# Grouped-query attention, 16 x 32 heads: 8 KB key pieces, score rows by key half, minima and sums joined on GpSimd

## The chip, the core and the metric

One core of one Trainium2 chip. The metric is device time of one execution in microseconds (us); the kernel before takes 350.31 us (median of 3 runs, 349.84 to 350.39). The core has TensorE (PE; PEld is its weight load), VectorE (DVE), ScalarE (ACT), GpSimd (POOL) and SyncE (SP), which issues all DMAs here. Each engine runs its own instructions in order; engines wait for each other by semaphores.

## The reference, cut to what matters

```python
B, Hq, Hkv, Sq, Sk, D = 16, 32, 8, 16, 2048, 128        # all bf16
k = jnp.repeat(k, rep, axis=1); v = jnp.repeat(v, rep, axis=1)     # rep = 4
scores = jnp.einsum("bhqd,bhkd->bhqk", q, k) * D ** -0.5
p = softmax(scores, axis=-1)
return jnp.einsum("bhqk,bhkd->bhqd", p, v)
```

There are 128 (batch, key head) groups. Each has 64 query rows (4 heads by 16 positions), 2,048 keys and 2,048 values of 128 numbers. K and V are 64 MB each, Q and the output 2 MB each; every byte of K and V is used once.

## The kernel before, in words

Work goes by *pairs* of groups, p = 0 to 63 (`NP`), 2 MB of K and V each. A pair passes through these steps; `[p % 2]` and the like are rotating buffers.

- **SP** issues, for t = 0, 1, 2 ...: `load_k(t)` (1 MB; for pair 0 two halves), a chunk of Q every eighth t (`load_q`, 256 KB, the queries of 8 pairs), `load_v(t - VLAG)`, `store(t - SLAG)` (L192-201). A K load waits until DVE has transposed the pair six before (`NK` = 6 buffers), a V load until the product eight before is done (`NV` = 8), a store until its output is normalised.
- **DVE** `kt` (L301): a 32x32-block transpose of K, two instructions of 128x1024 4-byte words a pair (a word is two bf16 numbers).
- **POOL** `spread` (L134) rearranges a chunk of Q once per 8 pairs; PE `queries` (L243) transposes it, ACT evacuates it to QT (L343); POOL copies one pair's part to Qs (L151).
- **PE** `scores` (L211): 32 matmuls of 32 rows by 64 columns into S_ps, which is all of four PSUM banks. PSUM rows 0-63 are group 0's queries, rows 64-127 group 1's; columns are keys.
- **DVE** Sneg (L324): one instruction over 128x2048 scales the scores by -scale, writes them to SBUF and leaves each row's minimum in nbias. Then `recip` of the row sum of the pair before.
- **ACT** exp (L353): one instruction over 128x2048 writes bf16 weights to P and the row sum to rowsum.
- **PE** `transposes` (L231): eight 128x128 transposes of P as 4-byte words; **ACT** copies them to PT in two halves (L363).
- **PE** `product` (L255): 16 matmuls with 128x128 weights and 256 moving columns (V of both groups), so half of each result (rows of one group by V of the other) is not used; **ACT** norm (L375) scales the two useful quarters, 64 rows each.

PE's order in a step p is `scores(p + 1)`, `product(p - PVLAG)`, `transposes(p)`, and in four of eight steps one unit of `queries` of the next chunk. ACT's order is exp p, norm p - PVLAG, the two PT copies of p, and a query evacuation where there is one. At the end, three products are left after the last scores; they go to the free S_ps banks.

Of the kernel before, what the change touches and what calls it, by code (L numbers as in the profile page):

```python
# [17 lines left out]
VLAG = 4  # L18
PVLAG = 3
# [4 lines left out]
def bass_standalone__gqa_softmax__sampling_kernel(  # L24
# [5 lines left out]
):  # L30
    B, Hq, Sq, D = q.shape
# [5 lines left out]
    J = Sk // 128  # L37
    assert J == 16 and NP % 8 == 0
# [8 lines left out]
    ident = sb("ident", [128, 128], BF16)  # L47
    ident4 = sb("ident4", [128, 128], F32)
    Kn = [sb(f"Kn{i}", [128, 2, J * 128], BF16) for i in range(NK)]
    Vb = [sb(f"Vb{i}", [128, 2, J, 128], BF16) for i in range(NV)]  # L50
    KT = [sb(f"KT{i}", [128, 2, J * 64], F32) for i in range(NKT)]
    Qn = [sb(f"Qn{i}", [128, 8, 128], BF16) for i in range(NQ)]
    Q4 = sb("Q4", [128, 8, 2, 4, 64], BF16)
    QT = [sb(f"QT{i}", [128, 4, 1024], BF16) for i in range(2)]
    Sneg = [sb(f"Sneg{i}", [128, Sk], F32) for i in range(2)]
    P = [sb(f"P{i}", [128, Sk // 2], F32) for i in range(2)]
    PT = [sb(f"PT{i}", [128, J // 2, 128], F32) for i in range(NPT)]
    Osb = [sb(f"O{i}", [128, 128], BF16) for i in range(NO)]
    nbias = sb("nbias", [128, NP], F32)
    rowsum = sb("rowsum", [128, NP], F32)  # L60
    rrec = sb("rrec", [128, NP], F32)

    Qs = [sb(f"Qs{i}", [128, 4, 128], BF16) for i in range(2)]
# [13 lines left out]
    sem_q4 = sem("sem_q4")  # L77
    sem_max = sem("sem_max")
    sem_rec = sem("sem_rec")
# [12 lines left out]
    kf = k.rearrange("b h s d -> (b h) (s d)").rearrange("g (a x) -> a g x", a=128)  # L92
# [3 lines left out]
    act_prog = []  # L96
    for i in range(4):
        act_prog.append(("qe", 0, i))
    for p in range(NP - 1):
        act_prog.append(("exp", p))  # L100
        if p >= PVLAG:
            act_prog.append(("norm", p - PVLAG))
        for h in range(2):
            act_prog.append(("pe", p, h))
        c, i = divmod(p, 8)
        if c + 1 < NQC and 2 <= i < 6:
            act_prog.append(("qe", c + 1, i - 2))
    act_prog.append(("exp", NP - 1))
    for p in range(NP - 4, NP - 2):
        act_prog.append(("norm", p))  # L110
    for h in range(2):
        act_prog.append(("pe", NP - 1, h))
    for p in range(NP - 2, NP):
        act_prog.append(("norm", p))

# [3 lines left out]

    def o_ap(p):  # L120
        if p < NP - 3:
            return O_ps[:, 0:256]
        x = p - (NP - 3)
        return S_ps[:, 512 * x:512 * x + 256]

    with nc.Block() as block:

        @block.gpsimd
        def _(gp):
            gp.iota(iota_t[:, :], [[1, 128]], base=0, channel_multiplier=-1).then_inc(sem_id, 1)  # L130
            gp.wait_ge(sem_id, 1)
            gp.tensor_scalar(ident[:, :], iota_t[:, :], 0.0, None, op0=ALU.is_equal).then_inc(sem_id, 1)
            gp.tensor_scalar(ident4[:, :], iota_t[:, :], 0.0, None, op0=ALU.is_equal).then_inc(sem_id, 1)
            def spread(c):  # L134
                gp.wait_ge(sem_q[c % NQ], 16 * (c // NQ + 1))
                if c >= 1:
                    gp.wait_ge(sem_tq, 4 * c)
                src = Qn[c % NQ][:, :, :].rearrange("p j (b x) -> p (j b) x", b=2)
                gp.tensor_copy(  # L139
                    Q4[:, :, :, :, :].rearrange("p j b r x -> p (j b) r x"),  # L140
                    src.unsqueeze(2).to_broadcast([128, 16, 4, 64]),
                ).then_inc(sem_q4, 8)

            spread(0)
            for p in range(NP):
                c, i = divmod(p, 8)
                if i == 0:
                    gp.wait_ge(sem_evq, 8 * c + 8)
                if p >= 2:
                    gp.wait_ge(sem_s, p - 1)  # L150
                gp.tensor_copy(Qs[p % 2][:, :, :], QT[c % 2][:, :, 128 * i:128 * (i + 1)]).then_inc(sem_qs, 1)  # L151
                if i == 0 and c + 1 < NQC:
                    spread(c + 1)

        @block.sync
        def _(sp):
            def load_k(p):
                s = p % NK
                if p >= NK:
                    sp.wait_ge(sem_kt, p - NK + 1)  # L160
                if p == 0:
                    for g in range(2):
                        sp.dma_start(Kn[s][:, g, :], kf[:, g, :]).then_inc(sem_k0[g], 16)
                else:
                    sp.dma_start(Kn[s][:, :, :], kf[:, 2 * p:2 * p + 2, :]).then_inc(sem_k[s], 16)

            def load_v(p):
# [7 lines left out]
                for x in range(2):  # L175
                    dst = Vb[s][:, :, 8 * x:8 * (x + 1), :].rearrange("a g j d -> a g (j d)")
                    src = vf[:, 2 * p:2 * p + 2, 1024 * x:1024 * (x + 1)]
                    sp.dma_start(dst, src).then_inc(sem_vl[x], 16)

            def load_q(c):  # L180
                s = c % NQ
                if c >= NQ:
                    sp.wait_ge(sem_q4, 8 * (c - NQ + 1))
# [3 lines left out]
            def store(p):  # L187
                s = p % NO
                sp.wait_ge(sem_nm, p + 1)
                sp.dma_start(of[128 * p:128 * (p + 1), :], Osb[s][:, :]).then_inc(sem_o[s], 16)  # L190

            for t in range(NP + SLAG + 1):  # L192
                if t < NP:
                    load_k(t)
                for c in range(NQC):
                    if t == max(0, 8 * c - QLEAD):
                        load_q(c)
# [8 lines left out]
        def _(pe):  # L206
# [4 lines left out]
            def scores(p, i, first=False):  # L211
# [4 lines left out]
                kt = KT[i % NKT][:, :, :].bitcast(BF16).rearrange("p g (t b x e) -> p g b e t x", t=J // 2, b=2, e=2)  # L216
                qs = Qs[i % 2]
                for acc in range(4):
                    b, e = divmod(acc, 2)
                    for r in range(4):  # L220
                        rows = slice(32 * r, 32 * (r + 1))
                        for g in range(2):
                            ins = pe.matmul(  # L223
                                S_ps[64 * g:64 * (g + 1), 512 * r:512 * (r + 1)],
                                qs[rows, acc, 64 * g:64 * (g + 1)],
                                kt[rows, g, b, e, :, :],
# [16 lines left out]
            def queries(p, i, first=False):  # L243
                if i == 0:
                    pe.wait_ge(sem_q4, p + 8)
                if i or not first:
                    pe.wait_ge(sem_evq, p + 2 * i)
                dst = stage_ap(2).bitcast(BF16)
                src = Q4[:, :, :, :, :].rearrange("p j b r (c e) -> p j b e (r c)", e=2)
                b, e = divmod(i, 2)  # L250
                for j in range(8):
                    ins = pe.transpose(dst[:, 128 * j:128 * (j + 1)], src[:, j, b, e, :], ident[:, :])  # L252
                ins.then_inc(sem_tq, 1)

            def product(p, i, out, tail=False, last=False):  # L255
# [5 lines left out]
                elif not isinstance(p, int) or p >= 1:  # L261
                    pe.wait_ge(sem_nm, p)
                pt = PT[i % NPT][:, :, :].bitcast(BF16).rearrange("p t (q e) -> p t e q", e=2)
                for j in range(J):
                    if last and j % 8 == 0:
                        pe.wait_ge(sem_vl[j // 8], 16)
                    ins = pe.matmul(  # L267
                        out, pt[:, j // 2, j % 2, :], Vb[i % NV][:, :, j, :],
                        start=(j == 0), stop=(j == J - 1),
                    )  # L270
                ins.then_inc(sem_pv, 1)

            def step(base, i, more=True):
                p = base + i
                if more:
                    scores(p + 1, i + 1)
                if not isinstance(base, int) or p >= PVLAG:
                    product(p - PVLAG, i - PVLAG, o_ap(0))
                transposes(p, i, first=isinstance(base, int) and p == 0)
                if (not isinstance(base, int) or base + 8 < NP) and 2 <= i < 6:  # L280
                    queries(base + 8, i - 2)

            for i in range(4):
                queries(0, i, first=True)
            scores(0, 0, first=True)
            for i in range(8):
                step(0, i)
            with pe.Fori(8, NP - 8, 8) as base:
                for i in range(8):
                    step(base, i)  # L290
            for i in range(7):
                step(NP - 8, i)
            for p in range(NP - 4, NP - 2):
                product(p, p, o_ap(p), tail=(p >= NP - 3))
            transposes(NP - 1, 7)
            for p in range(NP - 2, NP):
# [3 lines left out]
        def _(dve):  # L300
            def kt(p, g):  # L301
                if p == 0:
                    dve.wait_ge(sem_k0[g], 16)
                else:
                    dve.wait_ge(sem_k[p % NK], 16 * (p // NK + (1 if p % NK else 0)))
                ins = dve.transpose(  # L306
                    KT[p % NKT][:, g, :].rearrange("p (t b a e) -> p t e b a", t=J // 2, b=2, e=2),
                    Kn[p % NK][:, g, :].bitcast(F32).rearrange("p (t e b c) -> p t e b c", e=2, b=2, c=32),
                )
                if g == 1:  # L310
                    ins.then_inc(sem_kt, 1)

            def recip(p):
                dve.wait_ge(sem_exp, p + 1)
                dve.reciprocal(rrec[:, p:p + 1], rowsum[:, p:p + 1]).then_inc(sem_rec, 1)  # L315

            for p in range(2):
                for g in range(2):
                    kt(p, g)
            for p in range(NP):  # L320
                dve.wait_ge(sem_s, p + 1)
                if p >= 2:
                    dve.wait_ge(sem_exp, p - 1)
                dve.tensor_scalar(  # L324
                    Sneg[p % 2][:, :], S_ps[:, :], -scale, None,
                    op0=ALU.mult, op1=ALU.min, accum_out=nbias[:, p:p + 1],
                ).then_inc(sem_max, 1)
                if p >= 1:
                    recip(p - 1)
                if p + 2 < NP:  # L330
                    for g in range(2):
                        kt(p + 2, g)
            recip(NP - 1)
# [72 lines left out]
```

## Time and profile before

| | |
|---|---|
| median of 3 runs | 350.31 us |
| the profiled execution: time / span | 350.13 us / 348.3 us |
| busy: PE, DVE, ACT, POOL | 270.0, 294.8, 279.5, 68.5 us |
| moved by DMA | 138.70 MB, mean 398 GB/s |
| granted TensorE clock | full in all 40 slices |
| DVE, mean ns: K transpose 128x1024 / Sneg 128x2048 | 1223 / 2256 |
| ACT, mean ns: exp 128x2048 / PT copy 128x512 / query evacuation 128x1024 / norm 64x128 | 2003 / 595 / 1031 / 361 |

The span is what the profiler sees of one execution; the execution's own time is 1.8 us longer. A group's row gives the line, engine and operation, destination <- source with their shapes, the count, then total busy time and mean duration, then the idle time that the engine had just before these instructions and what ended it. "DMA share" is the mean busy share of the 16 DMA engines; it reads above 1 when packets overlap.

### The profile page before, as it was taken

How to read it: one execution, taken by the hardware profiler on the slowest of the kernel's cores; microseconds unless marked ns; L12 is line 12 of the kernel's file. 1: busy time of each engine (PE TensorE's matmuls, PEld its weight loads, DVE VectorE, ACT ScalarE, POOL GpSimd, SP SyncE). 2: the span in 40 equal slices, each digit the busy share in tenths (PEclk: the TensorE clock that was granted, in tenths of full speed). 3: DMA queues.
4: the chain of work that ended last, by engine and by line, in shares of the span. 5: the costliest groups of instructions: out<-in, count | busy, mean ns of one | idle time of the engine just before them, and what ended most of it. 6: DMA issues, size and time to landing. Idle time of an engine off the chain costs nothing.

```text
span 348.3 us, 9331 instructions
## 1 busy us (share of the span) xinstructions
PE 270.0 (78%) x3840; PEld 199.8 (57%) x3840; DVE 294.8 (85%) x320; ACT 279.5 (80%) x417; POOL 68.5 (20%) x79
## 2 busy tenths in 40 slices
PE   0338789988898989888867886778867868767776
PEld 0215566666666666666646655556645656556565
DVE  2229999999999999988989889889889879889850
ACT  0326899989998999899877997689986898777775
POOL 3251106110421124110331104201051101101000
PEclk9999999999999999999999999999999999999999
DMA  7999999999999999999999999999999999999991
GB/s 272 417 410 409 408 408 405 412 410 410 410 413 413 413 410 411 412 410 414 410 413 413 412 412 412 412 413 413 412 411 413 412 412 414 413 409 414 410 384 45
DMA packets 45494, 138.70 MB, mean 398 GB/s; under 512 B 11424, under 2 KB 11424, under 8 KB 45472
## 3 DMA queue, kind: packets, MB, share of 16 engines
q1 hardware_dynamic: 45472, 138.42, 100.0%
q8 instruction: 11, 0.18, 0.2%
q14 instruction: 11, 0.09, 0.1%
HBM read 136.31 MB, written 2.10 MB: 397 GB/s over the span
## 4 chain that ended last, share of the span: by engine, by line
DMA 40%; DVE 26%; issue 14%; PE 8%; SPq 6%; ACT 5%; POOL 1%; ACTq 0%; POOLq 0%
DMA Kn<-in_k_dram 38%; DVE KT L306 15%; DVE Sneg L324 11%; PE O_ps L267 3%; ACT P L353 3%; SPq L190 3%; SPq L173 3%; PE S_ps L223 2%; DMA Qn<-in_q_dram 2%; PE S_ps L267 2%; PE ST_ps L239 1%; ACT PT L363 1%; POOL Q L139 1%; ACT O L375 0%; DVE rrec L315 0%
## 5 line engine op out<-in xcount | busy, mean ns | idle before, releaser
L306 DVE STREAM_TRANSPOSE KT<-Kn 128x1024 f32<-128x1024 f32 x128 | 151.6, 1223 | 29.8 <-DMA Kn<-in_k_dram 29.8
L324 DVE TENSOR_SCALAR_CACHE_REDUCE Sneg<-S_ps 128x2048 f32<-128x2048 f32 x64 | 144.4, 2256 | 12.8 <-PE S_ps L223 12.8
L353 ACT ACTIVATE P<-Sneg,nbias 128x2048 bf16<-128x2048 f32 x64 | 128.2, 2003 | 11.9 <-DVE Sneg L324 10.9
L267 PE MATMUL O_ps<-Vb,PT 128*128 128x256 bf16 x976 | 117.2, 273 | 0.0
L223 PE MATMUL S_ps<-KT,Qs 32*64 32x512 bf16 x2048 | 73.6, 400 | 53.4 <-DVE Sneg L324 46.3
L267 PEld LDWEIGHTS O_ps<-Vb,PT 128*128 128x128 bf16 x976 | 90.6, 98 | 36.0 <-issue 25.0
L151 POOL COPY Qs<-QT 128x512 bf16<-128x512 bf16 x64 | 38.8, 613 | 234.5 <-PE S_ps L223 159.0
L239 PE MATMUL ST_ps<-ident,P 128*128 128x128 f32 x512 | 69.6, 280 | 6.5 <-ACT P L353 6.0
L363 ACT ACTIVATE PT<-ST_ps 128x512 f32<-128x512 f32 x128 | 69.7, 595 | 6.0 <-PE ST_ps L239 3.4
L223 PEld LDWEIGHTS S_ps<-KT,Qs 32*64 32x64 bf16 x2048 | 29.9, 104 | 76.9 <-issue 54.2
L375 ACT ACTIVATE O<-O_ps,rrec 64x128 bf16<-64x128 f32 x122 | 44.0, 361 | 31.7 <-PE O_ps L267 30.5
L239 PEld LDWEIGHTS ST_ps<-ident,P 128*128 128x128 f32 x512 | 57.6, 143 | 15.3 <-ACT P L353 13.6
L343 ACT ACTIVATE QT<-ST_ps 128x1024 bf16<-128x1024 bf16 x32 | 33.0, 1031 | 3.6 <-PE ST_ps L252 3.6
L252 PE MATMUL ST_ps<-ident,Q 128*128 128x128 bf16 x256 | 21.2, 230 | 15.7 <-POOL Q L139 10.9
L139 POOL COPY Q<-Qn 128x4096 bf16<-128x4096 bf16 x8 | 28.8, 3600 | 21.1 <-issue 16.2
L252 PEld LDWEIGHTS ST_ps<-ident,Q 128*128 128x128 bf16 x256 | 18.0, 103 | 16.8 <-issue 10.8
L315 DVE RECIPROCAL rrec<-rowsum 128x1 f32<-128x1 f32 x64 | 10.2, 159 | 3.4 <-ACT P L353 3.4
L353 ACT ACTIVATION_READ_ACCUMULATOR P<-Sneg,nbias 128x1 f32 x64 | 12.0, 187 | 0.0
L343 ACT ACT_TABLE_LOAD x1 | 1.3, 1283 | 12.0 <-PE ST_ps L252 12.0
L267 PE MATMUL S_ps<-Vb,PT 128*128 128x256 bf16 x48 | 5.6, 273 | 0.0
L324 DVE DVE_READ_ACCUMULATOR Sneg<-S_ps 128x1 f32 x64 | 5.4, 84 | 0.0
L267 PEld LDWEIGHTS S_ps<-Vb,PT 128*128 128x128 bf16 x48 | 4.7, 98 | 0.5
(8 smaller groups left out, 3.9 us busy)
## 6 DMA issues: line engine op xcount, KB each, us to landing
Kn<-in_k_dram SPq DMA_DIRECT2D x63, 1024.0 KB, 14.6
Vb<-in_v_dram SPq DMA_DIRECT2D x63, 1024.0 KB, 16.0
Qn<-in_q_dram SPq DMA_DIRECT2D x8, 256.0 KB, 13.9
out_dram<-O SPq DMA_DIRECT2D x64, 32.0 KB, 13.7
Kn<-in_k_dram SPq DMA_DIRECT2D x2, 512.0 KB, 3.9
Vb<-in_v_dram SPq DMA_DIRECT2D x2, 512.0 KB, 12.5
```

Source lines behind the costliest of these rows:

```text
L139: gp.tensor_copy(Q4[:, :, :, :, :].rearrange("p j b r x -> p (j b) r x"), src.unsqueeze(2).to_broadcast([128, 16, 4, 64]),).then_inc(sem_q ...
L151: gp.tensor_copy(Qs[p % 2][:, :, :], QT[c % 2][:, :, 128 * i:128 * (i + 1)]).then_inc(sem_qs, 1)
L223: ins = pe.matmul(S_ps[64 * g:64 * (g + 1), 512 * r:512 * (r + 1)], qs[rows, acc, 64 * g:64 * (g + 1)], kt[rows, g, b, e, :, :], start=(ac ...
L239: ins = pe.transpose(dst[:, 128 * t:128 * (t + 1)], P[i % 2][:, 128 * x:128 * (x + 1)], ident4[:, :])
L252: ins = pe.transpose(dst[:, 128 * j:128 * (j + 1)], src[:, j, b, e, :], ident[:, :])
L267: ins = pe.matmul(out, pt[:, j // 2, j % 2, :], Vb[i % NV][:, :, j, :], start=(j == 0), stop=(j == J - 1),)
L306: ins = dve.transpose(KT[p % NKT][:, g, :].rearrange("p (t b a e) -> p t e b a", t=J // 2, b=2, e=2), Kn[p % NK][:, g, :].bitcast(F32).rea ...
L324: dve.tensor_scalar(Sneg[p % 2][:, :], S_ps[:, :], -scale, None, op0=ALU.mult, op1=ALU.min, accum_out=nbias[:, p:p + 1],).then_inc(sem_max, 1)
L343: act.activation(QT[c % 2][:, i, :].rearrange("p (a j) -> p a j", j=8), stage_ap(2).bitcast(BF16).rearrange("p (j a) -> p a j", j=8), ACT. ...
L353: act.activation(P[p % 2][:, :].bitcast(BF16).rearrange("p (t r x) -> p t r x", t=8, r=4), Sneg[p % 2][:, :].rearrange("p (r t x) -> p t r ...
L363: act.activation(PT[p % NPT][:, 4 * h:4 * (h + 1), :].rearrange("p t q -> p (t q)"), stage_ap(h), ACT.Copy,).then_inc(sem_ev[h], 1)
L375: ins = act.activation(Osb[p % NO][rows, :], o_ap(p)[rows, 128 * g:128 * (g + 1)], ACT.Copy, scale=rrec[rows, p:p + 1])
```

## The change

1. **K layout.** A K load takes 8 KB per partition (32 keys of one group) in place of two pieces of 4 KB; a partition holds keys of one group only (partitions 0-63 group 0, 64-127 group 1). `kt` is one instruction over 2,048 words.
2. **Score rows.** PSUM rows 0-63 are now key half 0 of a query and rows 64-127 key half 1; the column halves are the two groups. A query's minimum and sum thus lie in two rows, 64 partitions apart.
3. **Sneg and exp in two halves** (one per group), each with its own accumulator. Sneg now also reorders: four streams interleaved, so consecutive elements are written 16 bytes apart. exp reads and writes in plain order.
4. **`exchange` on POOL**: two small copies across partitions, two `min` that make nbias, and two `add` that make rowsum of the pair before, with semaphores between them; exp now waits for POOL (`sem_b`), not for DVE.
5. **Products**: 32 matmuls with 64 weight columns and 128 moving columns, one group to each half of the output rows; norm is one instruction over 128 rows.
6. **Queries** as 4-byte words: 16 transposes a chunk, not 32, evacuated in four 128x512 pieces, in two steps of eight. Q chunk 0 is loaded first of all; POOL and DVE spread it in two quarters each, later chunks go in quarters on POOL; the first chunk uses four PSUM places rather than one.
7. **Order and lags**: V comes six pairs behind K (was four), products run four pairs behind (was three); `recip` handles two pairs at once; the last V load is split 12 to 4 of 16 (was 8 to 8); ACT runs one tiny exp at the start, which adds one to `sem_nm`.

```diff
-VLAG = 4
-PVLAG = 3
+VLAG = 6
+PVLAG = 4
...
-    kf = k.rearrange("b h s d -> (b h) (s d)").rearrange("g (a x) -> a g x", a=128)
+    kf = k.rearrange("b h s d -> (b h s d)").rearrange("(r x) -> r x", x=4096)
...
+            gp.memset(warm[:, :], 0.0).then_inc(sem_id, 1)
...
+            def exchange(p):
+                x = slice(0 if p < NP else 2, 4 if p else 2)
+                if p < NP:
+                    gp.wait_ge(sem_max, p + 1)
+                if p:
+                    gp.wait_ge(sem_exp, p)
...
+                gp.tensor_copy(oth[lo, p, x], own[hi, p, x]).then_inc(sem_x, 1)
+                gp.wait_ge(sem_x, 2 * p + 1)
+                gp.tensor_copy(oth[hi, p, x], own[lo, p, x]).then_inc(sem_x, 1)
+                gp.wait_ge(sem_x, 2 * p + 2)
+                if p < NP:
+                    for h in range(2):
+                        ins = gp.tensor_scalar(nbias[:, p, h:h + 1], own[:, p, h:h + 1], oth[:, p, h:h + 1], None, op0=ALU.min)
+                    ins.then_inc(sem_b, 1)
+                if p:
+                    for h, rows in enumerate((lo, hi)):
...
+                        gp.tensor_tensor(
+                            rowsum[rows, p - 1:p], own[rows, p, 2 + h:3 + h], oth[rows, p, 2 + h:3 + h], op=ALU.add,
+                        ).then_inc(sem_sum, 1)
...
+            for p in range(NP):
+                c, i = divmod(p, 8)
+                exchange(p)
+                if p + 2 < NP:
+                    queries(p + 2)
+                if c + 1 < NQC and i < 4:
...
+                    spread(gp, c + 1, i).then_inc(sem_q4, 2)
+            exchange(NP)
...
-                    sp.dma_start(Kn[s][:, :, :], kf[:, 2 * p:2 * p + 2, :]).then_inc(sem_k[s], 16)
+                    sp.dma_start(Kn[s][:, :], src).then_inc(sem_k[s], 16)
...
+            load_q(0)
             for t in range(NP + SLAG + 1):
                 if t < NP:
                     load_k(t)
...
-                for j in range(J):
-                    if last and j % 8 == 0:
-                        pe.wait_ge(sem_vl[j // 8], 16)
-                    ins = pe.matmul(
-                        out, pt[:, j // 2, j % 2, :], Vb[i % NV][:, :, j, :],
-                        start=(j == 0), stop=(j == J - 1),
-                    )
+                for j in range(16):
+                    w, t, e = j // 8, j % 8 // 2, j % 2
+                    if last and j in (0, 12):
+                        pe.wait_ge(sem_vl[j // 12], 16)
+                    for h in range(2):
+                        ins = pe.matmul(
+                            out[64 * h:64 * (h + 1), :], pt[:, h, w, t, e, :], Vb[i % NV][:, h, j, :],
+                            start=(j == 0), stop=(j == 15),
+                        )
...
+                scores(p + 1, i + 1)
                 if more:
-                    scores(p + 1, i + 1)
-                if not isinstance(base, int) or p >= PVLAG:
+                    queries(start, 2 * (i % 8 - 4))
+                if not known or p >= PVLAG:
                     product(p - PVLAG, i - PVLAG, o_ap(0))
-                transposes(p, i, first=isinstance(base, int) and p == 0)
...
+                transposes(p, i, first)
+                if more:
+                    queries(start, 2 * (i % 8 - 4) + 1)
...
-            for p in range(NP - 4, NP - 2):
-                product(p, p, o_ap(p), tail=(p >= NP - 3))
+            for p in range(NP - 5, NP - 3):
+                product(p, p, o_ap(p), tail=(p >= NP - 4))
             transposes(NP - 1, 7)
-            for p in range(NP - 2, NP):
+            for p in range(NP - 3, NP):
                 product(p, p, o_ap(p), tail=True, last=(p == NP - 1))
...
+            dve.wait_ge(sem_q[0], 16)
+            for u in range(2, 4):
+                spread(dve, 0, u).then_inc(sem_q4d, 2)
...
-                dve.tensor_scalar(
-                    Sneg[p % 2][:, :], S_ps[:, :], -scale, None,
-                    op0=ALU.mult, op1=ALU.min, accum_out=nbias[:, p:p + 1],
-                ).then_inc(sem_max, 1)
-                if p >= 1:
-                    recip(p - 1)
+                for h in range(2):
+                    ins = dve.tensor_scalar(
+                        Sneg[p % 2][:, 1024 * h:1024 * (h + 1)].rearrange("p (t g l f) -> p t f g l", t=4, g=2, f=4),
+                        S_ps[:, 1024 * h:1024 * (h + 1)].rearrange("p (g t f l) -> p t f g l", g=2, t=4, f=4),
+                        -scale, None, op0=ALU.mult, op1=ALU.min, accum_out=own[:, p, h:h + 1],
+                    )
+                ins.then_inc(sem_max, 1)
+                if p >= 3 and p % 2:
+                    recip(p - 3, 2)
                 if p + 2 < NP:
-                    for g in range(2):
-                        kt(p + 2, g)
...
+                    kt(p + 2)
...
-                    act.wait_ge(sem_max, p + 1)
+                    act.wait_ge(sem_b, p + 1)
...
+                    for h in range(2):
+                        x = slice(1024 * h, 1024 * (h + 1))
+                        ins = act.activation(
+                            P[p % 2][:, :].bitcast(BF16)[:, x], Sneg[p % 2][:, x], ACT.Exp,
+                            bias=nbias[:, p, h:h + 1], scale=-1.0, accum_out=own[:, p + 1, 2 + h:3 + h],
+                        )
+                    ins.then_inc(sem_exp, 1)
```

## The prediction

> **What bounds the kernel now.** I read the page's head first, then busy time by stage, the groups, and the timeline of the end.
>
> ```profile
> span 348.3 us, 9331 instructions
> DMA  7999999999999999999999999999999999999991
> GB/s 272 417 410 409 408 408 405 412 410 410 410 413 413 413 410 411 412 410 414 410 413 413 412 412 412 412 413 413 412 411 413 412 412 414 413 409 414 410 384 45
> ```
>
> All DMA engines are full from the second slice to the next to last, whatever the compute engines do. So the bound is DMA, plus a lead-in and a tail.
>
> ```profile
> 100.00:142.00 42.00, 38.78 (x555) 28.25 (x550) 41.77 (x46) 40.02 (x59) 9.62 (x11) 1.00 1.03 412
> 310.00:320.00 10.00, 7.39 (x112) 5.49 (x110) 8.92 (x11) 7.81 (x12) 1.23 (x2) 1.00 1.03 410
> 340.00:348.30 8.30, 5.61 (x52) 4.87 (x49) 0.16 (x1) 4.55 (x12) 0.00 (x0) 0.99 0.15 40
> ```
>
> The columns after the length are busy PE, PEld, DVE, ACT, POOL, then clock, DMA share, GB/s. At 100 to 142 us DVE was busy 41.77 of 42 us with 46 instructions, five a pair: 4.57 us a pair, its own pace, while it made up a late start (first Sneg at 23.65). By 310 it waits for K. DMA's pace is 2.163 MB a pair (2 MB of K and V, Q's and the output's 32 KB each) by 412.5 GB/s = 5.24 us.
>
> ```profile
> L306 DVE STREAM_TRANSPOSE KT<-Kn 128x1024 f32<-128x1024 f32 x128 | 151.6, 1223 | 29.8 <-DMA Kn<-in_k_dram 29.8
> L324 DVE TENSOR_SCALAR_CACHE_REDUCE Sneg<-S_ps 128x2048 f32<-128x2048 f32 x64 | 144.4, 2256 | 12.8 <-PE S_ps L223 12.8
> L353 ACT ACTIVATE P<-Sneg,nbias 128x2048 bf16<-128x2048 f32 x64 | 128.2, 2003 | 11.9 <-DVE Sneg L324 10.9
> L267 PE MATMUL O_ps<-Vb,PT 128*128 128x256 bf16 x976 | 117.2, 273 | 0.0
> ```
>
> The timeline of the end:
>
> ```profile
> 329.00 2.37 DVE L306 STREAM_TRANSPOSE KT<-Kn 128x1024 f32<-128x1024 f32 x2 [0.92 <-DMA Kn<-in_k_dram]
> 334.89 2.29 DVE L324 TENSOR_SCALAR_CACHE_REDUCE Sneg<-S_ps 128x2048 f32<-128x2048 f32 x1 [1.25 <-PE S_ps L223]
> 338.58 2.00 ACT L353 ACTIVATE P<-Sneg,nbias 128x2048 bf16<-128x2048 f32 x1
> 341.95 3.66 PE L267 MATMUL S_ps<-Vb,PT 128*128 128x256 bf16 x32
> 345.65 0.74 ACT L375 ACTIVATE O<-S_ps,rrec 64x128 bf16<-64x128 f32 x2 [1.01 <-PE S_ps L267]
> ```
>
> K 63 landed at 329.0. The last V load ended at about 341.6 (packet records), 12.6 us behind it. But pair 63's scores, exp and transposes took until 342, so two products were still to do: 6.7 us of tail after the last byte, 3.9 of them compute behind the data.
>
> **The change, part by part.**
>
> *8 KB pieces.* The packet records give medians of 9 ns (4 B), 18 (256 B), 84 (2,048 B), 159 (4,096 B): 9 ns plus 27.3 bytes a ns. K needs 512 packets fewer per engine (64 MB / 16 / 4 KB = 1,024, now 512). Bounds: 512 x 9 = 4.6 us, and 0 if a piece is handled as two. Packets overlap, so the net price is smaller: a pair has 5.24 us for 44 packets an engine (32 of K and V, 8 of output, 1 of Q, 3 that signal) and 135 KB, which is 4.95 us at 27.3; the other 0.29 us is 6.6 ns a packet. I take 512 x 6.6 = **-3.4 us**. DMA's pace becomes 5.19 us a pair. [...]
>
> *V two pairs later, products one later; last V cut 12 to 4.* Between K 63 and the end of DMA there are now V 57 to 63, seven loads of 2.6 us = 18 us, not 12.6. Counting from K 63: transpose to 2.3, Sneg 62 to 4.7, scores 63 and Sneg 63 to 8.5, exchange to 9.6 (below), exp to 12.2, transposes and PT copies to 14. All is done before the last V, and products 61 and 62 run as their V lands. After the last quarter of V 63: product 0.25 (four of 16 steps) to 1.2 us (product 62 still before it at 1.9 us each); I take 1.0. Then norm 0.4, store 1.5 (346.0 to 347.5 before), end of span 0.8: 3.7 in place of 6.7, **-3.0 us** (-2.5 to -4.0).
>
> *Q first, first chunk in four places, exp table early.* Q lands near 3.6 us (the first K half, twice as large, was in use at 4.24), spread to 5.8 (0.9 us a quarter, 3.6 / 4), transposed and evacuated to about 8, Sneg 0 near 11 rather than 23.65. Worth 0 here (+-0.5): DMA was full anyway. K's first piece lands 0.6 us later, behind Q in SP's queue; the earlier compute covers it. DVE's two quarter spreads (1,024 elements, up to 1.05 us each) run while K 0 is on its way. If the lead were gone, DVE would be late at the end as below.
>
> *DVE.* From recip (1 element, 159 ns) and Sneg (2,048, 2,256) an element costs 1.02 ns and an instruction 0.16 us. Two halves: 2 x 1.21 + 2 x 0.08 for the accumulators = 2.42 to 2.58, against 2.27 from Sneg to recip now: +0.15 to +0.31. One K transpose for two: 2.25 against 2.27. recip every other pair: -0.08. So 4.57 becomes 4.65 to 4.8; I take **4.75**, under 5.19: nothing on the path. The new 16-byte step of its writes is costed at nothing, because K's transpose writes at 8-byte steps at full pace and ACT's query evacuation reads at 256-byte steps (1,031 ns for 1,024); neither is this case, so it is a rival.
>
> *exchange.* POOL's tiny operations: 0.10 us (MEMSET 128x1), 0.19 (fixed part of its copies: 3,600 ns for 4,096, 613 for 512), at most 0.53 (TENSOR_SCALAR 128x128). Two copies, two minima and three semaphore steps of 0.1 (iota's end to the next start): 0.7 to 2.4 us, taken as 1.1 by the copies. exp p is that much later, but Sneg p + 2 has 8 us until it needs exp p done, and ACT has norm and two PT copies to do meanwhile. Behind the waiting POOL are Qs of p + 2 (0.61) and a quarter spread (0.9), both wanted a pair later. POOL's total is some 2.9 us a pair. Cost 0.
>
> *ACT.* Copies of 512 (595) and 1,024 (1,031) give 0.85 ns an element; exp in halves is 2 x (1.13 + 0.19) = 2.63 against 2.19; norm one for two: -0.38; query pieces of 512: 4 x 0.44 / 8 = -0.22. From 4.37 to 4.2 us a pair, off the path.
>
> *PE.* Products: 1.87 us a pair now; 32 matmuls of half length at the same pace 1.9; as low as 1.1 (the scores' 32 matmuls and loads), as high as 3.1 if every load (98 ns) shows. 4.2 us a pair, 5.4 at worst. SP's order: V goes behind two more K loads, stores stay; product p waits for a V that lands right behind K p + 6, in the step in which DVE takes that K. Counted from the landing of that K: V at 2.6, product done at 4.5, transposes (1.04) at 5.6, the next scores (1.11) at 6.8. DVE meanwhile does the K transpose, a Sneg and, from the next K at 5.2, another transpose, until 7.4; so the scores are there in time. A unit of queries (four transposes, 0.55) in two steps of eight uses up most of the 0.6 us left there.
>
> Sum: -3.4 - 3.0 = -6.4 us on 348.3 = 341.9; the execution's own time has 1.8 us more (350.13 beside 348.3, and 350.31 the median of the runs): **343.7**. Its own range is 341.3 (-4.6, -4.0, 0.2) to 346.
>
> **Rivals.**
>
> *Only the tail gains.* The engines handle 8 KB as two 4 KB pieces: 350.13 - 3.0 = 347.1. For: no data packet here is larger than 4 KB. Against: instruction fetches of 8,192 B are in the records, the quickest at 309 ns, 9 below two of 159.
>
> *DVE becomes the bound (slower).* From the first Sneg at 11 us, 62 pairs at pace x and then about 18.5 us (two last Snegs and scores 6.2, exchange 1.1, exp 2.6, transposes 1.1, three products 5, norm and store 2.5) must fit 341.9: it decides at x = 5.04, Sneg 0.29 us a pair dearer than I take it. If each write at a 16-byte step takes double, Sneg costs 2.1 more, x = 6.85, and 11 + 425 + 18.5 + 1.8 = 456 us; at a quarter dearer, x = 5.28, 359. For: no row shows such a step. [...]
>
> *A stall in the loop.* V just in time, slow product loads (PE 5.4 a pair) or an exchange of 2.4 us behind exp's 2.63 puts 0.1 to 0.15 us a pair on the last half or all of it: 3 to 10 us, 347 to 353. For: V's lead over its product falls from seven steps to six. Against: every loop reckoned above stays under 5.19.
>
> **Chances.** Forecast 0.58, only the tail 0.13, a stall 0.11 (a third faster, a fifth the same), DVE bound 0.18. The range 341.0 to 351.0 holds the first two and most of the third and leaves out DVE's case. About 0.2% (0.7 us) can be told from no change: faster 0.58 + 0.13 + 0.04 = 0.75, same 0.02, slower 0.23.
>
> **What would show it.** K's packets at 309 ns and steady slices near 416 GB/s; Sneg halves at 1.2 us; DVE idle behind K from about a third of the span on; the last product within 1.2 us of the last V. Wrong if DVE shows no idle time before the end, or if DMA's row falls below 9.

## The result and the profile after

The changed kernel takes **404.96 us** (median of 4 runs, 404.08 to 406.8) against 350.08 for the kernel before beside it: ratio 1.157, 95% interval 1.154 to 1.161. It is 55 us slower where 6 to 7 us less were forecast. The profiled execution's span is 403.2 us.

The head of the page after: span, then busy tenths of DVE, the granted clock, DMA share and GB/s in 40 slices.

```profile
span 403.2 us, 11846 instructions
...
DVE  4999999999999999999999999999999999999960
...
PEclk9656898969988796979979898998989899898998
DMA  8999999999999999999999999999999999974600
GB/s 286 421 416 413 412 412 416 414 416 408 370 363 386 351 351 373 344 381 373 350 357 372 376 347 365 359 382 353 367 357 344 379 347 342 375 273 170 213 9 20
```

From the second to the tenth slice DMA runs at its own pace, 408 to 421 GB/s. Then it falls to some 360: the six K buffers are full, and a K load waits for DVE's transpose. In the queue's own waits (SPq is SyncE's queue of DMA issues; us in total, times, longest):

```profile
SPq L221 <- DVE KT L382: 219.9, 57, 5.2
```

DVE is at 9 from the second to the 38th slice. The stages (length; busy PE, PEld, DVE, ACT, POOL; clock; DMA share; GB/s) say the same:

```profile
100.00:142.00 42.00, 27.77 (x537) 19.38 (x520) 42.00 (x40) 27.31 (x51) 17.02 (x55) 0.88 0.98 368
300.00:342.00 42.00, 26.02 (x524) 18.30 (x522) 42.00 (x41) 28.13 (x54) 16.75 (x53) 0.96 0.97 356
```

DVE was busy 42.00 of 42 us in both; before, it had gaps by 310 us. PE and ACT have slack. Of the prediction's two signs of being wrong, DVE without idle time came; DMA's row stayed at 9 until the 35th slice. The busy share hides DMA's waits: by the packet records the 8 KB packets took 311 ns in the mean at 50 to 92 us and 364 at 100 to 142, with a median of 309 in both: a few long packets keep the share up. The groups on which the sum rested:

```profile
L399 DVE TENSOR_SCALAR_CACHE_REDUCE Sneg<-S_ps 128x1024 f32<-128x1024 f32 x128 | 247.3, 2020 | 1.3 <-PE S_ps L284 1.3
L434 ACT ACTIVATE P<-Sneg,nbias 128x1024 bf16<-128x1024 f32 x128 | 146.0, 1141 | 101.3 <-POOL nbias L181 101.3
L382 DVE STREAM_TRANSPOSE KT<-Kn 128x2048 f32<-128x2048 f32 x63 | 147.4, 2340 | 1.3 <-DMA Kn<-in_k_dram 1.3
```

A Sneg half over 1,024 elements takes 2,020 ns; the whole of 2,048 took 2,256 before. DVE's sequence of one pair, from the timeline:

```profile
202.81 2.02 DVE L399 TENSOR_SCALAR_CACHE_REDUCE Sneg<-S_ps 128x1024 f32<-128x1024 f32 x1
204.68 0.15 DVE L399 DVE_READ_ACCUMULATOR Sneg<-S_ps 128x1 f32 x1
204.68 1.99 DVE L399 TENSOR_SCALAR_CACHE_REDUCE Sneg<-S_ps 128x1024 f32<-128x1024 f32 x1
206.52 0.15 DVE L399 DVE_READ_ACCUMULATOR Sneg<-S_ps 128x1 f32 x1
206.52 2.31 DVE L382 STREAM_TRANSPOSE KT<-Kn 128x2048 f32<-128x2048 f32 x1
208.75 1.97 DVE L399 TENSOR_SCALAR_CACHE_REDUCE Sneg<-S_ps 128x1024 f32<-128x1024 f32 x1
```

From start to start: 1.87, 1.84 and 2.23 us, together 5.94 us a pair, over the 5.19 forecast for DMA. The first Sneg starts at 12.03 us and pair 62's at 381.66: 369.6 / 62 = 5.96 us a pair.

### The profile page after: what moved, and what is told of

Read it like the earlier page. It is cut to its first block, busy times and chain, and to the rows that moved or that the text cites. A ratio compares the mean times of both kernels' runs of the same rounds, so it can differ in the third digit from the quotient of the medians.

```text
span 403.2 us, 11846 instructions
## 1 busy us (share of the span) xinstructions
PE 257.1 (64%) x4736; PEld 179.3 (44%) x4736; DVE 384.0 (95%) x356; ACT 258.2 (64%) x482; POOL 148.6 (37%) x487
## 4 chain that ended last, share of the span: by engine, by line
DVE 83%; issue 10%; DMA 2%; PE 2%; ACT 2%; POOL 1%; SPq 0%; ACTq 0%; DVEq 0%; POOLq 0%
DVE Sneg L399 54%; DVE KT L382 29%; DMA Kn<-in_k_dram 2%; ACT P L434 2%; PE S_ps L333 1%; POOL nbias L181 1%; PE ST_ps L300 0%; PE S_ps L284 0%; SPq L219 0%; POOL oth L175 0%; POOL oth L177 0%; DVE rrec L387 0%; SPq L241 0%; ACT O L454 0%; DVEq L397 0%
## 5 line engine op out<-in xcount | busy, mean ns | idle before, releaser
L399 DVE TENSOR_SCALAR_CACHE_REDUCE Sneg<-S_ps 128x1024 f32<-128x1024 f32 x128 | 247.3, 2020 | 1.3 <-PE S_ps L284 1.3
L434 ACT ACTIVATE P<-Sneg,nbias 128x1024 bf16<-128x1024 f32 x128 | 146.0, 1141 | 101.3 <-POOL nbias L181 101.3
L382 DVE STREAM_TRANSPOSE KT<-Kn 128x2048 f32<-128x2048 f32 x63 | 147.4, 2340 | 1.3 <-DMA Kn<-in_k_dram 1.3
L175 POOL COPY oth<-own 64x4 f32<-64x4 f32 (+1 forms) x65 | 11.9, 183 | 221.3 <-DVE Sneg L399 219.2
L333 PEld LDWEIGHTS O_ps<-Vb,PT 128*64 128x64 bf16 x1920 | 64.1, 122 | 27.7 <-issue 27.7
L333 PE MATMUL O_ps<-Vb,PT 128*64 128x128 bf16 x1920 | 74.2, 238 | 0.0
L181 POOL TENSOR_SCALAR nbias<-own,oth 128x1 f32<-128x1 f32 x128 | 34.0, 281 | 6.4
L144 POOL COPY Q<-Qn 128x1024 bf16<-128x1024 bf16 x30 | 31.5, 1051 | 1.7 <-DMA Qn<-in_q_dram 1.7
L187 POOL TENSOR_TENSOR rowsum<-own,oth 64x1 f32<-64x1 f32 x128 | 23.8, 186 | 5.1
L454 ACT ACTIVATE O<-O_ps,rrec 128x128 bf16<-128x128 f32 x60 | 21.2, 353 | 3.8 <-PE O_ps L333 3.2
L177 POOL COPY oth<-own 64x4 f32<-64x4 f32 (+1 forms) x65 | 11.8, 181 | 4.0
```

The costliest lines, as they stand in the source:

```text
L144: return eng.tensor_copy(Q4[:, 4 * jh:4 * jh + 4, b, :, :], src.unsqueeze(2).to_broadcast([128, 4, 4, 64]))
L181: ins = gp.tensor_scalar(nbias[:, p, h:h + 1], own[:, p, h:h + 1], oth[:, p, h:h + 1], None, op0=ALU.min)
L187: gp.tensor_tensor(rowsum[rows, p - 1:p], own[rows, p, 2 + h:3 + h], oth[rows, p, 2 + h:3 + h], op=ALU.add,).then_inc(sem_sum, 1)
L333: ins = pe.matmul(out[64 * h:64 * (h + 1), :], pt[:, h, w, t, e, :], Vb[i % NV][:, h, j, :], start=(j == 0), stop=(j == 15),)
L382: ins = dve.transpose(dst, src)
L399: ins = dve.tensor_scalar(Sneg[p % 2][:, 1024 * h:1024 * (h + 1)].rearrange("p (t g l f) -> p t f g l", t=4, g=2, f=4), S_ps[:, 1024 * h:1 ...
```

## The experiments

The question was why Sneg's halves cost 0.8 us more than reckoned. Three theories: the **write** step (neighbouring elements written 16 bytes apart), the **read** order (runs of 32 from two banks in turn), or something beside Sneg's patterns (a fixed cost of halves with accumulators, or the busier GpSimd). Ratios are against runs of the kernel before, taken beside each experiment.

**Sneg in plain order.**

```diff
-  Sneg[...1024 half].rearrange("p (t g l f) -> p t f g l", t=4, g=2, f=4),
-  S_ps[...1024 half].rearrange("p (g t f l) -> p t f g l", g=2, t=4, f=4),
+  Sneg[...1024 half],
+  S_ps[...1024 half],
```

> The changed kernel with Sneg read and written in plain order in both halves; the reordering of the scores is left out, all else stays. Write theory (elements written 16 bytes apart are what costs) and read theory (the PSUM read hops between two banks every 32 elements): a Sneg half takes 1.2 to 1.3 us in place of 2.01, DVE 4.75 us a pair, DMA becomes the bound again, 341 to 347 us. Fixed-cost theory (two instructions with an accumulator each cost some 0.8 us more) or GpSimd theory (DVE is held up by the busier GpSimd): a half stays at 1.9 to 2.0 us and the time near 405.

Measured: 344.71 us, ratio 0.986 (0.981 to 0.990). Halves, accumulators and GpSimd are as in the changed kernel, so none of these three is the cause by itself. The tile's rows (least, median and greatest ns; first and last start):

```profile
L399 DVE TENSOR_SCALAR_CACHE_REDUCE Sneg<-S_ps x128: 1183/1219/1225, 12.4 to 326.5; 128x1024 f32<-128x1024 f32 x128
L399 DVE DVE_READ_ACCUMULATOR Sneg<-S_ps x128: 81/84/88, 13.6 to 327.7; 128x1 f32 x128
```

**Only the 16-byte write step.**

```diff
+  Sneg[...].rearrange("p (t x f) -> p t f x", t=4, f=4),
+  S_ps[...].rearrange("p (t f x) -> p t f x", t=4, f=4),      # this read is plain
```

> The changed kernel with Sneg read in plain order but still written 16 bytes apart (runs of 64 elements, four interleaved); which score lands where differs from the reference's order. Write theory: a half stays at 1.9 to 2.0 us, 400 to 407 us. Read theory: 1.2 to 1.3 us, 341 to 347 us. If both share the cost: in between, 1.5 to 1.7 us and 360 to 385 us.

Measured: 406.92 us, ratio 1.158 (1.153 to 1.164), with

```profile
L399 DVE TENSOR_SCALAR_CACHE_REDUCE Sneg<-S_ps x128: 1910/2031/2148, 13.8 to 391.6; 128x1024 f32<-128x1024 f32 x128
```

The write step alone brings all of the loss.

**Only the read order.**

```diff
+  Sneg[...].rearrange("p (t f g l) -> p t f g l", t=4, g=2, f=4),   # written plain
   S_ps[...].rearrange("p (g t f l) -> p t f g l", g=2, t=4, f=4),
```

> The changed kernel with Sneg read as the change reads it (runs of 32 elements, alternately from two banks) but written in plain order; the interleaving is left out. Write theory: a half takes 1.2 to 1.3 us, 341 to 347 us. Read theory: it stays at 1.9 to 2.0 us, 400 to 407 us.

Measured: 343.83 us, ratio 0.984 (0.979 to 0.989):

```profile
L399 DVE TENSOR_SCALAR_CACHE_REDUCE Sneg<-S_ps x128: 1183/1219/1227, 12.9 to 327.1; 128x1024 f32<-128x1024 f32 x128
```

The read order costs nothing. Nor does a pattern of short runs as such: the runs are of 32 elements here and of 64 in the run before.

**A write step of 8 bytes** (two streams, not four; the edit of the 16-byte run with f=2).

> The changed kernel with Sneg read in plain order and written 8 bytes apart (two streams interleaved, not four); the order of the scores is not the reference's. [...] Write theory without a threshold (any gap costs): 1.5 to 2.0 us, 360 to 405 us.

Measured: 344.41 us, ratio 0.984 (0.981 to 0.987):

```profile
L399 DVE TENSOR_SCALAR_CACHE_REDUCE Sneg<-S_ps x128: 1185/1220/1229, 13.0 to 326.9; 128x1024 f32<-128x1024 f32 x128
```

So not every gap costs: a half takes 1,220 ns at 8 bytes, 1,219 in plain order and 2,031 at 16. The price of DVE's 4-byte writes begins above 8 bytes, at 16 at the latest. Steps of 12 bytes or of more than 16 were not run, and why it begins there no run shows.

**The same edit in the kernel before** (`"p (t x f) -> p t f x", t=8, f=4` on Sneg's destination).

> The kernel before with one edit: Sneg written 16 bytes apart (read in plain order; which score lands where differs from the reference's order). Write theory: Sneg takes 3.8 to 4.0 us in place of 2.26, the pair 4.57 + 1.65 = 6.2 us on DVE; from its first Sneg at 23.6, 62 pairs and a tail of about 17 us: 420 to 430 us. Theory that the write step costs only beside something else of the change (halves, GpSimd): under 355 us.

Measured: 416.57 us, ratio 1.190 (1.189 to 1.192), 3.4 us under the expectation's lower end:

```profile
L324 DVE TENSOR_SCALAR_CACHE_REDUCE Sneg<-S_ps 128x2048 f32<-128x2048 f32 x64 | 246.1, 3845 | 13.0 <-PE S_ps L223 13.0
```

With 0.16 us for the instruction itself, as in the prediction, an element costs (3,845 - 160) / 2,048 = 1.80 ns here, (2,020 - 160) / 1,024 = 1.82 ns in the changed kernel, and 1.02 ns before: 1.8 times, with or without the rest of the change.

**Where else could the interleaving go?** First to exp's write:

```diff
-  P[...half], Sneg[...half], ACT.Exp,
+  P[...half].rearrange("p (t g l f) -> p t f g l", t=4, g=2, f=4),
+  Sneg[...half].rearrange("p (g t f l) -> p t f g l", g=2, t=4, f=4), ACT.Exp,
```

> The changed kernel with the interleaving moved from Sneg to exp: Sneg plain in and out, exp reads Sneg in runs of 32 and writes its bf16 weights four streams interleaved, 8 bytes apart. Every element lands where the change puts it. Threshold theory (two writes to 16 bytes are free, on ACT as on DVE): exp stays at 1.14 us a half, Sneg 1.21, 343 to 346 us. Theory that ACT pays for any gap in its writes: exp 1.9 us a half, ACT 4.05 + 1.57 of other work = 5.7 us a pair, over DMA's 5.19: 375 to 385 us.

Measured: four runs of 471.76 to 481.38 us; by the two fastest, ratio 1.354 (1.349 to 1.359), beyond either expectation. A half of exp took 2,586 ns in the median. To tell exp's write from its read:

```diff
+  P[...half].rearrange("p (t y f) -> p t f y", t=4, f=4),
+  Sneg[...half].rearrange("p (t f y) -> p t f y", t=4, f=4), ACT.Exp,   # this read is plain
```

> The changed kernel with Sneg plain, and exp reading in plain order but writing bf16 8 bytes apart (the order of the weights is not the reference's). Theory that ACT's 2-byte writes 8 bytes apart made exp 2.59 us a half: it stays there, 470 to 480 us. Theory that it was exp's read in runs of 32: 1.14 us, 343 to 346 us.

Measured in a single run: 478.42 us.

```profile
L434 ACT ACTIVATE P<-Sneg,nbias 128x1024 bf16<-128x1024 f32 x128 | 317.2, 2587 | 6.1 <-POOL nbias L181 6.1
```

It is ACT's write: 2,587 ns for a half, against 1,141 in the changed kernel. The 8 bytes that are free to DVE's 4-byte writes (1,220 ns a half against 1,219) are not free to ACT's 2-byte ones.

Then to TensorE:

```diff
-  "p (w x b l f) -> p w b f x l", w=2, x=16, b=2, l=32)
+  "p (w t x b l f) -> p w b f t l x", w=2, t=4, x=4, b=2, l=32)     # moving columns
```

> The changed kernel with the interleaving moved into the score matmuls: they take the K columns in such an order (256 bytes between neighbours in fours, where it was 4) that the scores come out interleaved, and Sneg copies runs of 128. Every element lands where the change puts it. If TensorE reads its moving columns at any step: scores 1.1 us, Sneg 1.21 a half, 343 to 345 us. If it pays as DVE's writes do (1.8 times): scores 2.0 us, behind the K transpose's 2.3, PE at 4.5 us a pair: 343 to 348 us. If it pays four times: scores 4.4 us, and with Sneg's 2.5 in turn 7.1 us a pair: 460 us or more.

Measured: 455.97 us, ratio 1.304 (1.300 to 1.307). A score matmul took 1,045 ns in the median, 383 in the kernel before, and a pair's scores 3.9 us, 3.5 times the 1.11 of the kernel before: nearest to the last of the three cases, and a little under it in time. One pair's scores took 3.89 us from 205.21 us on. It is not the clock: the mean granted clock of the run was 0.898 against 1.00 before, and the quickest of its score matmuls took 1,042 ns against 380, 2.7 times.

```profile
L284 PE MATMUL S_ps<-KT,Qs 32*64 32x512 bf16 x2048 | 248.0, 1083 | 22.0 <-DVE Sneg L399 20.6
L399 DVE TENSOR_SCALAR_CACHE_REDUCE Sneg<-S_ps 128x1024 f32<-128x1024 f32 x128 | 151.7, 1223 | 139.6 <-PE S_ps L284 139.6
```

DVE's idle time (139.6 us) now ends with the scores.

Last to Sneg's read of PSUM. The matmuls keep runs of 32 columns but in the order (f, t); then the read needs a step of 512 bytes in fours, and the write is in plain runs of 128:

```diff
-  "p (w x b l f) -> p w b f x l", w=2, x=16, b=2, l=32)
+  "p (w t x b l f) -> p w b f x t l", w=2, t=4, x=4, b=2, l=32)
...
-  Sneg[...].rearrange("p (t g l f) -> p t f g l", t=4, g=2, f=4),
-  S_ps[...].rearrange("p (g t f l) -> p t f g l", g=2, t=4, f=4),
+  Sneg[...].rearrange("p (t g l f) -> p g t l f", t=4, g=2, f=4),
+  S_ps[...].rearrange("p (g f t l) -> p g t l f", g=2, t=4, f=4),
```

> The changed kernel with the interleaving moved to Sneg's read: the score matmuls keep runs of 32 columns in another order, Sneg reads PSUM 512 bytes apart in fours and writes SBUF in plain runs of 128. Every element lands where the change puts it. If DVE's read of PSUM has no such price (ACT's query evacuation read PSUM 256 bytes apart at 1,031 ns for 1,024): Sneg 1.2 us a half, scores 1.1 us, 343 to 345 us, 1.5 to 2% under the kernel before. If DVE pays for steps on either side: 2.0 us a half or more, 400 us or more.

Measured: **344.94 us**, ratio 0.987 (0.985 to 0.989). It computes all of the reference and beats both kernels. Its profiled execution, 343.42 us, has

```profile
span 341.6 us, 11846 instructions
...
DMA  7999999999999999999999999999999999999994
...
L399 DVE TENSOR_SCALAR_CACHE_REDUCE Sneg<-S_ps 128x1024 f32<-128x1024 f32 x128 | 149.8, 1205 | 3.1 <-PE S_ps L284 3.0
L382 DVE STREAM_TRANSPOSE KT<-Kn 128x2048 f32<-128x2048 f32 x63 | 145.4, 2307 | 24.5 <-DMA Kn<-in_k_dram 24.5
```

and DMA is the bound again: DVE idles 24.5 us behind K.

**The two gains of the sum, each by itself.** K's 8 KB pieces in the kernel before:

```diff
-  sp.dma_start(Kn[s][:, :, :], kf[:, 2 * p:2 * p + 2, :])
+  sp.dma_start(Kn[s][:, :, :].rearrange("a g x -> a (g x)"), k8[128 * p:128 * (p + 1), :])
```

> The kernel before with K loaded in 8 KB pieces from pair 1 on (so the keys sit in other places than its later steps take them from); nothing else. The step of the sum as made: 3.4 us less, 346.5 to 347.3 us. By one fixed 9 ns a packet: 4.6 less, 345.5 to 346. [...] No gain, if DVE and PE at the end hide it: 350.

Measured: 345.48 us (345.25 to 345.69), ratio 0.987 (0.986 to 0.989): 4.50 us less. Pair 0 keeps its pieces of 4 KB, so 504 packets an engine are saved, not the 512 of the prediction: 8.9 ns for each. The packet records have a median of 309 ns for 8,192 bytes, 9 less than two of 4,096.

V six behind K in the kernel before (`VLAG = 6`, nothing else):

> The kernel before with V six pairs behind K (VLAG 6, PVLAG 3 as before). As the tail was reckoned: K 63 lands 5.2 us earlier against the last V, so pair 63 is done before it and only the last product, norm and store remain: 2.0 to 3.5 us less, 346.8 to 348.3 us. Rival: with one pair less between a V and its product, PE waits for V in the steady part and the time is 350 or more.

Measured: 350.72 us (12 runs), ratio 1.0017 (1.0007 to 1.0027): no gain. The waits of this kernel (engine, line, whom it waited for; us, times, longest):

```profile
PEld O_ps L267 <- issue: 66.2, 52, 2.7
PE O_ps L267 <- issue: 36.9, 30, 2.2
...
DVE Sneg L324 <- PE S_ps L223: 31.5, 37, 11.7
...
PE O_ps L267 <- DMA Vb<-in_v_dram: 8.8, 8, 1.4
DVE KT L306 <- DMA Kn<-in_k_dram: 7.6, 2, 4.1
```

Before, PE sat idle ahead of none of its product matmuls (0.0 in their group), DVE waited 12.8 us for scores and 29.8 us for K. Here PE idles ahead of products (36.9 us of it ended by nothing that the waits show, 8.8 by V), and DVE's wait has moved from K to the scores behind them. The landing times in the trace tell what the 36.9 us are: each of the 37 idle times of over 0.2 us ahead of a product, 45.6 us together, ends within 0.15 us of the landing of that product's V. Pair 63 is then no earlier: its exp starts at 339.69 us, at 338.58 before.

And V four behind in the 344.94 us kernel:

> The kernel of f5_psum_read with V four pairs behind K again (VLAG 4; products stay four behind). If the tail was reckoned rightly: K 63 lands only 12.6 us ahead of the last V, transposes 63 end at 14 us, and three products of 1.05 us follow, so the last product ends about 4.5 us behind the last V rather than 1: 1.5 to 3.5 us more than f5_psum_read, 346 to 348.5 us. If V six behind makes PE wait for V in the steady part, as b3_before_lag6 suggests, and that reaches the end: no more than f5_psum_read, 342 to 345 us.

Measured: 346.88 us, ratio 0.992 (0.991 to 0.994), against 0.987 with V six behind. The lag is worth 1.9 us there (346.88 - 344.94). The end with V four behind:

```profile
337.93 2.87 PE L333 MATMUL S_ps<-Vb,PT 128*64 128x128 bf16 x96
...
340.85 0.37 ACT L454 ACTIVATE O<-S_ps,rrec 128x128 bf16<-128x128 f32 x1 [0.53 <-PE S_ps L333]
```

and of the 344.94 us kernel, V six behind:

```profile
337.39 1.08 PE L333 MATMUL S_ps<-Vb,PT 128*64 128x128 bf16 x32 [0.91 <-DMA Vb<-in_v_dram]
338.51 0.37 ACT L454 ACTIVATE O<-S_ps,rrec 128x128 bf16<-128x128 f32 x1 [1.63 <-PE S_ps L333]
```

The last load data ended at 337.56 and 337.49 us (packet records), so the same. With four, three products (96 matmuls) are still to do at that time; with six, one, and it waits for its V. V comes just in time here too: 46 products wait for it for over 0.2 us, 68.0 us in all. But DVE's wait for scores is 3.0 us, not 31.5 as in the kernel before with that lag, so the wait does not reach DVE.

## Why the prediction was wrong, by its own steps

**The step that failed** is in the DVE part: "The new 16-byte step of its writes is costed at nothing, because K's transpose writes at 8-byte steps at full pace and ACT's query evacuation reads at 256-byte steps". Both rows are in the profile (1,223 ns for a K transpose of 1,024 words, 1,031 ns for a query evacuation), and neither bears on it: the 8-byte run shows that 8 bytes are on the free side (1,220 ns a half against 1,219), and the PSUM-read run that reads of PSUM 512 bytes apart are free too (1,218). A write to SBUF 16 bytes apart took 2,020. By durations the step cost 2 x (1.82 - 1.02) x 1.024 = 1.6 us a pair in Sneg. From start to start it cost 1.4, because consecutive instructions overlap by 0.1 to 0.2 us, as the starts above show: pairs in which DVE never idled took 4.54 us in the read-order run and 5.96 in the changed kernel. So the forecast of 4.75 without a price for the step was 0.2 too high, and the step's own price of 1.4 was the term that was missing.

**The rival that came true** is "DVE becomes the bound", with its place, its condition (5.04 us a pair) and, by its formula, its time: 12.0 + 62 x 5.96 + 18.5 + 1.8 = 401.8 against 405.0 for the profiled execution; its end took 21.5 us (381.66 to 403.2), not 18.5. It had 0.18; its two prices, a quarter dearer (359) and double (456), stood on either side of the 1.8 times that was measured. No run shows the doubling that the second price takes: an element cost 1.82 ns at 16 bytes, 1.02 before. The range left it out.

The size of the gap does not set the price by itself: ACT's bf16 writes 8 bytes apart took 2,587 ns a half in place of 1,141, where DVE's 4-byte writes 8 bytes apart took 1,220 in place of 1,219.

**The other steps**, by the runs without the write step:

- *Time without it*: forecast 343.7, measured 344.71, 343.83, 344.41 and 344.94. That these are so close is in part luck: the next parts were off in both directions.
- *8 KB pieces*: -3.4 forecast by a net price of 6.6 ns a packet; measured -4.5 us, 8.9 ns a packet. The upper bound of 4.6, the whole 9 ns, was the right one: taking off the overlap of packets was the error of size. This also rules out the rival by which only the tail gains. (The quickest 8 KB packet of the kernel before took 307 ns; the prediction has 309.)
- *Tail*: 3.7 us behind the last V forecast, 4.1 measured in the 344.94 us kernel (341.6 - 337.5). Before it was 7.0 (348.3 - 341.3 by the packet records; the prediction took 341.6 and 6.7). But V six behind gave nothing by itself in the kernel before; it needs other parts of the change. The product at 1.09 us rather than 1.92 is the likely one, which no run isolates. The stall that was reckoned as a rival, V just in time, is what the kernel before shows with that lag.
- *Sum*: the two parts as measured would make 4.5 + 2.9 = 7.4 us; the difference of the 344.94 us kernel to the one before is 5.1 us in the medians and 6.7 in the profiled executions, and its last load ends 0.7 us later than with 8 KB pieces alone (337.5, 336.8). What keeps these 0.7 to 2.3 us was not settled.
- *DVE's other terms*: a plain half 1.22 (1.21 forecast), K transpose 2.31 (2.25).
- *exchange*: exp starts 1.16 us after the last Sneg instruction of its pair (379.52 to 380.68 in the changed kernel; 1.1 forecast), and it is not on the path before the end.
- *ACT*: exp half 1.14 (1.13), norm 0.35 (0.36). *PE*: product 1.09 us where the granted clock was 1.00 (207.90 to 209.00 us of the changed kernel; 1.9 forecast, 1.1 its lower bound).
- *Q first*: first Sneg at 12.0 us (11 forecast, 23.65 before); no run isolates what it is worth. It counts where DVE is the bound: the rival's formula begins with it.

## What to carry to other kernels

Cost an access pattern by a row with the same engine, the same side (read or write, SBUF or PSUM) and the same step; a row that differed in one of these was no bound here (8 bytes apart: DVE's writes 1,220 ns a half against 1,219, ACT's 2,587 against 1,141), and an engine with 10% of slack must not be given an uncosted pattern on its longest instruction. When data must be interleaved, the free place here was the read of PSUM (1,218 ns a half): the same permutation cost 60 us and more on DVE's write, ACT's write or TensorE's moving side. V six pairs behind K made V come just in time in the kernel before and in the 344.94 us kernel (products waited 45.6 and 68.0 us for it); it helped, by 1.9 us, only in the second, where DVE waited 3.0 us for scores and not 31.5.

## What the runs showed of the hardware that was not expected

- DVE, 4-byte writes to SBUF: 1.02 ns an element in plain order or 8 bytes apart, 1.8 ns 16 bytes apart; the accumulator read behind it also grew, from 84 to 172 ns in the median.
- ACT, 2-byte writes 8 bytes apart: 2,587 ns for 1,024 elements against 1,141.
- TensorE, moving columns 256 bytes apart in fours: 1,045 ns a matmul of 512 columns against 383.
- DVE, PSUM reads 512 bytes apart in fours: no price (1,218 ns in the median against 1,219).
- The granted TensorE clock was 0.88 at 100 to 142 us of the changed kernel (PE busy 27.77 us) and 1.00 in the kernel before (38.78 us). PE's idle time alone does not explain it: it was 1.00 at 300 to 330 us of the 344.94 us kernel with PE busy 19.20 of 30 us, and 0.898 in the mean of the matmul-order run, where DVE idled 139.6 us behind PE's scores. A pair's scores took 1.93 us where the clock was 0.50 (200.80 to 202.75 us of the changed kernel) and 1.11 in other pairs. DVE covered it, so it did not set the time.
